# A fused RWKV-5 and tanh-shrink kernel: who issues the first loads, and a planner that counts the two halves' ports

## The chip, the cores and the metric

The kernel runs on one core of one Trainium2 chip. A core has TensorE (PE), VectorE (DVE), ScalarE (ACT), GpSimd (POOL) and SyncE (SP), each with its own queue of instructions in order. Transfers between memory and SBUF are issued here by SP, ACT and POOL and moved by 16 DMA engines. The metric is the device time of one launch in microseconds (us); lower is better.

## The reference

A linear attention with a decaying state, for 4 batches, 8 heads, 768 steps and heads of 48, and then a layer of hidden width 2048 on its 3072 rows of 384:

```python
for t in range(S):
    cur = einsum('bhd,bhe->bhde', u[None] * kt, vt)
    y[:, :, t] = einsum('bhd,bhde->bhe', rt, state + cur)
    state = w[None, :, :, None] * state + einsum('bhd,bhe->bhde', kt, vt)
x = y.transpose(0, 2, 1, 3).reshape(3072, 384)
h = x @ w_in            # 384 x 2048
g = h - tanh(h)
out = g @ w_out         # 2048 x 384
```

r, k, v, w and u are float32. w_in and w_out are float64: the kernel gets them as 64-bit integers and makes float32 of them itself.

## The kernel before

**Units.** The attention is cut into 24 units of 64 steps and two batches; unit n works on steps 64 (n // 2) and on batches 0, 1 or 2, 3. The first batch of a unit lies on SBUF partitions 0 to 63, the second on 64 to 127. `fetch` loads each of r, k and v in two transfers, one for each half (`z` 0 and 1), of 96 KB in runs of 192 bytes. A unit then goes through these steps: PE turns r and k (`turn`, L763), DVE and ACT scale or copy them (`rT` L767, `kT` L771 or L776), PE multiplies them (`levels`, L717), DVE copies the product under a mask into `at` (`x.cp`, L919), ACT writes the diagonal (L788) from `du` (DVE, L780, L909, L784), PE makes the outputs and the new state (`outputs`, `to_state`), ACT takes the outputs into `xt` and `rest` (L855), and DVE updates the state (L882, L928). `kw` (L894) is k with a decay.

A head has 48 numbers and takes 64 partitions, so 16 rows of each half are left; three of the eight heads' worth of output is put there. That is done by copies: POOL's six transfers `xt<-rest` (`fill`, L876) for each pair of units, the "fills". A pair of units makes one block j of 256 rows.

**Hidden tiles.** For each block j, the layer runs in tiles of 256 hidden columns (`hidden`): PE computes h in two groups of six matmuls (L168), ACT makes five functions of it (L177 to L185), DVE combines them to g (L192 to L198), and PE multiplies g by w_out (L206, or L257 in a form with seven products that POOL's sums L242 to L246 and DVE's `mixed` L266 prepare). The first six blocks go through the weights in three passes of 4, 4 and 8 column groups, so that the first hidden tiles need few weights: 12 tiles on the first four weight pieces, 12 on the next four, and 24 on the rest.

**Weights.** There are 16 pieces (w_in and w_out in turn, two of each: n = 0, 1 of w_in, 2, 3 of w_out, and so on), each 768 KB as loaded into one of four staging tiles `st`. A w_out piece is one transfer by SP. A w_in piece comes in four parts: 48 rows at partition 0, 16 rows at 48, 48 rows at 64 and 16 rows at 112. SP loads the two parts of 48 rows, POOL the two of 16 (L123). Five DVE (L137, L138, L141 to L143) and two ACT instructions (L139, L140) convert a piece; the staging tile is then free for the piece four later.

**The planner.** Everything in the main part is a task with an engine, a cost in us, the tasks it must follow and a due time (`add`). `Plan.order` first sets due times backwards from the dependences and then changes them at random many times; each time `forward` lays all tasks out on the engines by these costs, and the change is kept if the laid-out end is no later. In the first part of the search only the time up to `BUSY` is laid out. The instructions are then issued in the order that results, so a cost in the planner moves no instruction's duration, only the order on each queue. For transfers `forward` has one channel that serves them one after the other (`data` us each), a time from issue to landing of at least `LANDS`, `LANDED` after the channel, and 8 transfers under way on each queue (`LANES`). Where PE would wait at the start, dummy matmuls (`fills`, L655) are put in.

Of the kernel before, what the change touches and what calls it, by code (L numbers as in the profile page):

```python
# [33 lines left out]
AHEAD = 2  # L34
# [266 lines left out]
class Plan:  # L301
# [6 lines left out]

    HOP, NEAR_HOP, LANDS, LANDED, LANES, EARLY, SPARE, WARM, SLOW = 0.16, 0.06, 2.4, 1.6, 8, 45.0, 20.0, 6.0, (60.0, 3.0)
    AHEAD, BUSY = 0.05, 240.0  # L310
    CHUNK, CHUNK_0, ASKED, COMES, FIRST = 256, 192, 55, 3.4, 9.5
# [4 lines left out]

    def add(self, engine, cost, run, after=(), due=1e9, data=0, gated=False, steps=0):
        t = SimpleNamespace(engine=engine, cost=cost, run=run, after=[x for x in after if x], due=due, data=data,
                            gated=gated, steps=steps, then=[], n=len(self.tasks))
        for x in t.after:  # L320
            x.then.append(t)
        self.tasks.append(t)
        return t
# [12 lines left out]
    def forward(self, due, until=1e9):  # L336
# [3 lines left out]
        waiting = self.queues(ready, count)  # L340
        free, lanes, channel = dict(self.BEGIN), {}, 0.0
        step, bound, comes, fills = 0, self.CHUNK_0, 0.0, iter(self.fills)
# [3 lines left out]
        while len(done) < len(ready):  # L346
# [40 lines left out]
            if t.data:  # L387
                channel = max(channel, start + 1.2) + t.data
                end = max(end + self.LANDS, channel + self.LANDED) + self.slow(start)
                lanes[e] = lanes[e][1:] + [end]  # L390
# [58 lines left out]

    def order(self, first=2500, tries=500):  # L450
# [12 lines left out]
        def moved():  # L463
            by, at, wide = chance.choice((0.3, 1, 2, 5)), chance.uniform(0, until), chance.choice((15, 40, 100, 700))
            return [x + chance.gauss(0, by) * (start is not None and abs(start - at) < wide / 2) for x, start in zip(due, plan[1])]


        until = self.BUSY
        plan = self.forward(due, until)
        for _ in range(first):  # L470
            new = moved()
            other = self.forward(new, until)
            if other[0] <= plan[0]:
                plan, due = other, new
# [41 lines left out]
def near(ctx, tc, r, k, v, w, u, out, shared, moe_w_in, moe_w_out):  # L516
# [136 lines left out]
    def fills(to):  # L653
# [20 lines left out]
    doubled = add("ACT", .6, lambda: A.copy(twice, inverse[:, :, None, 1:].to_broadcast([128, NP, 2, SHORT])), [now])  # L674
    now = tabled = add("PE", .7, table, [doubled], steps=8)
    downs = add("ACT", .5, lambda: A.copy(w_down, tab.rearrange("s (h d) -> s h d", h=H)[:, :, :D]), [now])
# [6 lines left out]
        out=ub.rearrange("p h d -> p (h d)"),  # L683
        in_=bass.AP(tensor=u.tensor, offset=u.offset, ap=[[0, 128], [1, H * D]])), data=.7)

# [15 lines left out]
    for n in range(weights.count):  # L701

        queues, data = (("SP",), (3.0,)) if n % 4 > 1 else (("SP", "POOL") * 2, (1.2, .95) * 2)
        of = [add(e, .55, lambda n=n, i=i, e=e: weights.load(n, i, e_of[e]), [converted[n - 4] if n >= 4 else None],
                  data=x, gated=True) for i, (e, x) in enumerate(zip(queues, data))]
# [15 lines left out]
    def unit(n):  # L721
# [21 lines left out]
        direct = j == 0  # L743

        def fetch(name, src, after):
            def run(z):
                if name == "k" and not hasattr(t, "kt"):
                    t.kt = first_k[slot] if direct else load.tile([128, H, D], F32, name="kt", tag="kt")
                to = {"r": rt, "v": vt}.get(name)
                Q.dma_start(out=(t.kt if to is None else to)[HALF[z], :, :D],  # L750
                            in_=src[half * 2 + z, :, steps_at, :].rearrange("h t d -> t h d"))

            of = [add("SP", .65, lambda z=z: run(z), after, data=.71) for z in range(2)]
            return add("none", 0, lambda: None, of)
# [135 lines left out]
        if two:  # L890
            free = [b1.xt, b1.rest, b1.add, b1.cp, b1.diag]
        turns, turned = .46, 16
        x.turn = add("PE", turns, lambda: turn(rt, r_ps), [x.r] + free, steps=turned)
# [9 lines left out]
        if product:  # L903
            now = add("ACT", 1.05, own_k, [x.kT, w_us])
            x.own = add("PE", .7, own_levels, [now, x.rT, b2.out], steps=64)
            x.diag = add("DVE", .64, lambda: V.copy_predicated(t.at, same.bitcast(I32)[:, None, None, :].to_broadcast([128, 2, NP, SHORT]), own_lev), [x.own, b2.out])
# [7 lines left out]
        if two:  # L914
            now = add("PE", .66, from_state, both + [x.rT, b1.xt, b1.rest, b1.add, b2.decay, x.kT], steps=64)
            begun = [add("ACT", .15, between, [now])]
        x.lev = add("PE", .7 if two else (1.33 if swap else 1.73) if ch else .7, levels,
                    begun + [x.kT, x.rT, b2.out] + ([b2.decay, b1.xt, b1.rest, b1.add] if ch else []), steps=128 if ch and not two else 64)
        x.cp = add("DVE", .64, lambda: V.copy_predicated(t.at, before, lev), [x.lev, b2.out] + ([] if product else [x.diag]))  # L919
        x.out = now = add("PE", .95 if direct else 1.21, outputs,  # L920
                          [x.cp, x.diag, x.v, b1.xt, b1.rest, b1.add] + ([x.extra] if direct else [x.kw]), steps=96 if direct else 128)
        if direct:
            now = x.out = add("PE", .55, to_state, [now, x.kw], steps=64)
# [3 lines left out]
        x.add = add("DVE" if ch else "ACT", .47 if ch else 1.2, keep, [x.out, x.rest, x.xt]) if more else None  # L927
        x.decay = x.add if not ch else add("DVE", .47, lambda: V.tensor_tensor(state[:, :, :, :D], state[:, :, :, :D], w_all, ALU.mult), [x.add]) if more else None  # L928
        if direct:
            filled.setdefault((j, "all"), []).append(x.xt)  # L930
        elif slot == L - 1:
            filled[j, "all"] = [add("POOL", .52, lambda i=i, kk=kk: fill(i, kk), [x.rest, x.xt], data=.1)
                                for kk in range(NK) for i in range(2)]
# [17 lines left out]
    def finished_seven(t, x, half, due, pace):  # L951
# [9 lines left out]
        for i in (1, 0):  # L961
            now = steps[4 if i else 6]
            if t.fs[0]:
                now = add("DVE", .47, lambda i=i: dense.gather(t, i), [now], due + 3 * pace)
            stored[j, i] = [add("POOL", .6, lambda z=z, i=i: dense.store(t.os[i], L * j + i, z, G), [now], due + 4 * pace, data=.4)
                            for z in range(2)]

    def hidden(j, fs, f, due, pace, seven=False):
# [40 lines left out]
        for i in range(L):  # L1009
# [7 lines left out]
            if whole and j < d.NB - 1:  # L1017

                stored[j, i] = [add("POOL", .6, lambda z=z, i=i, ends=ends: dense.store(ends.o, L * j + i, z, G),
                                    [x.empty[-1]], due + 4 * pace, data=.4) for z in range(2)]  # L1020

# [339 lines left out]
```

## Time and profile before

| | before |
|---|---|
| runs | 603.26, 606.02 and 605.67 us, median 605.67 |
| profiled execution | 607.26 us, of which the span from first to last instruction is 605.5 |
| busy PE, DVE, ACT, POOL | 582.4, 466.4, 403.3, 201.0 us |
| mean granted TensorE clock | 0.989 |
| DMA | 33.78 MB in 86326 packets, 78536 of them under 512 B |

"Busy" is time in which an engine executes something. An engine that waits is not busy, but PE's matmuls are pipelined with modelled ends, so a busy PE may be waiting between them. DMA share is the mean share of time in which the 16 DMA engines had a packet under way. "A <- B" in a list of waits means that A stood idle until B let it go. Six matmuls of h at full clock take 1.29 us when they follow each other closely, and 1.49 to 1.56 when a group stands alone.

### The profile page before, as it was taken

To read this page: it belongs to the slowest core of one execution; us is meant where nothing else is said; L and a number is where in the kernel's file an instruction comes from. 1 tells how busy PE (TensorE), PEld (TensorE's weight loads), DVE (VectorE), ACT (ScalarE), POOL (GpSimd) and SP (SyncE) were. 2 spreads that over 40 slices of the span, in tenths; PEclk is the share of its full clock that TensorE was granted. 3 is DMA by queue.
4 is the path that set the end of the run, shared out by engine and by line. 5 is a ranking of instruction groups with operands and counts; after the bars stand their busy time and mean duration, and the time that the engine had idled before them with its cause. 6 is when DMAs were issued, how large, how long until landed. Compare 5 with 4: busy or idle time off the path is not lost.

```text
span 605.5 us, 14670 instructions
## 1 busy us (share of the span) xinstructions
PE 582.4 (96%) x5781; PEld 485.7 (80%) x5781; DVE 466.4 (77%) x782; ACT 403.3 (67%) x902; POOL 201.0 (33%) x366
## 2 busy tenths in 40 slices
PE   8877999999999999999999999999999999999996
PEld 4555767667777669999999999888889889889995
DVE  6699699999999999867677776767765775555666
ACT  3677699899866676655556686465866676565652
POOL 5002212021000123544455473425334435334540
PEclk9889899999999999999999999999999999999999
DMA  6966585967300210110111020122201100100101
GB/s 125 228 126 126 113 194 99 143 167 124 105 14 0 48 28 14 26 27 1 28 27 26 2 60 1 41 41 48 53 16 34 41 2 8 29 2 8 26 3 30
DMA packets 86326, 33.78 MB, mean 56 GB/s; under 512 B 78536, under 2 KB 80680, under 8 KB 86248
## 3 DMA queue, kind: packets, MB, share of 16 engines
q1 hardware_dynamic: 81084, 25.57, 21.1%
q0 software_dynamic: 4992, 6.99, 5.5%
q8 instruction: 47, 0.77, 0.5%
q14 instruction: 31, 0.25, 0.2%
q10 hardware_dynamic: 172, 0.20, 0.1%
HBM read 26.94 MB, written 4.72 MB: 52 GB/s over the span
## 4 chain that ended last, share of the span: by engine, by line
PE 76%; DVE 6%; DMA 5%; ACT 4%; issue 4%; SPq 3%; POOL 1%; DVEq 0%; ACTq 0%; POOLq 0%
PE h L168 37%; PE p L257 26%; PE o L206 6%; PE yk_ps L717 4%; SPq L750 3%; DMA st<-in_moe_w_in_dram 2%; DMA xt<-rest 1%; PE yk_ps L763 1%; POOL xt L876 1%; DMA st<-in_moe_w_out_dram 1%; DVE rT L767 1%; DVE at L919 1%; ACT s L177 1%; DVE tg L194 1%; DVE g L198 1%
## 5 line engine op out<-in xcount | busy, mean ns | idle before, releaser
L168 PE MATMUL h<-xt,w_in_sb 128*128 128x256 f32 x1152 | 285.7, 385 | 2.7 <-DMA xt<-rest 2.7
L168 PEld LDWEIGHTS h<-xt,w_in_sb 128*128 128x128 f32 x1152 | 214.6, 192 | 35.9 <-issue 2.1
L242 POOL TENSOR_TENSOR sg<-g 128x256 f32<-128x256 f32 x69 | 52.1, 755 | 176.7 <-DVE g L198 152.2
L257 PE MATMUL p<-mixed,sg 128*128 128x192 f32 x426 | 104.1, 326 | 0.0
L192 DVE TENSOR_TENSOR g<-h,th 128x512 f32<-128x512 f32 x96 | 65.8, 686 | 48.9 <-ACT s L177 23.0
L194 DVE SCALAR_TENSOR_TENSOR tg<-s,tg 128x512 f32<-128x512 f32 x96 | 71.1, 741 | 36.6 <-ACT tg L181 20.0
L181 ACT ACTIVATE tg<-h 128x512 f32<-128x512 f32 x96 | 57.2, 596 | 58.5 <-PE h L168 56.9
L179 ACT ACTIVATE th<-h 128x512 f32<-128x512 f32 x96 | 57.4, 598 | 39.1 <-PE h L168 39.0
L177 ACT ACTIVATE s<-h 128x512 f32<-128x512 f32 x96 | 57.4, 598 | 37.3 <-PE h L168 37.2
L876 POOL DMA_DIRECT2D xt<-rest x66 | 32.5, 499 | 146.3 <-ACT rest L855 145.8
L257 PEld LDWEIGHTS p<-mixed,sg 128*128 128x128 f32 x426 | 75.0, 190 | 0.3 <-issue 0.3
L198 DVE COPY_PREDICATED g<-small,tg 128x512 f32<-128x512 int32 x96 | 71.1, 741 | 4.7 <-DVE tg L196 0.5
L257 PE MATMUL p<-w_out_sb,g 128*128 128x192 f32 x284 | 71.9, 335 | 1.1 <-DVE at L919 1.1
L196 DVE SCALAR_TENSOR_TENSOR tg<-q,tg 128x512 f32<-128x512 f32 x96 | 67.5, 703 | 6.4 <-ACT q L183 2.4
L206 PE MATMUL o<-w_out_sb,g 128*128 128x384 f32 x192 | 71.3, 495 | 0.1
L183 ACT ACTIVATE q<-s,m1b 128x512 f32<-128x512 f32 x96 | 69.8, 727 | 0.6
L185 ACT ACTIVATE small<-s,smallb 128x512 f32<-128x512 f32 x96 | 69.6, 725 | 0.3
L257 PEld LDWEIGHTS p<-w_out_sb,g 128*128 128x128 f32 x284 | 51.8, 190 | 9.0 <-DVE at L919 1.5
L788 ACT ACTIVATE at<-same,du 128x64 f32<-128x64 f32 x184 | 47.9, 343 | 2.8 <-DVE du L784 2.6
L206 PEld LDWEIGHTS o<-w_out_sb,g 128*128 128x128 f32 x192 | 35.2, 190 | 15.8 <-DVE g L198 0.2
L246 POOL TENSOR_TENSOR sg<-sg,g 128x128 f32<-128x128 f32 x69 | 41.0, 594 | 5.1
L244 POOL TENSOR_TENSOR sg<-sg,g 128x128 f32<-128x128 f32 x69 | 36.6, 530 | 5.2
(133 smaller groups left out, 672.3 us busy)
## 6 DMA issues: line engine op xcount, KB each, us to landing
st<-in_moe_w_out_dram SPq DMA_DIRECT2D x8, 768.0 KB, 4.5
rt<-in_r_dram SPq DMA_DIRECT2D x48, 96.0 KB, 2.9
vt<-in_v_dram SPq DMA_DIRECT2D x48, 96.0 KB, 3.4
st<-in_moe_w_in_dram SPq DMA_DIRECT2D x16, 288.0 KB, 5.5
kt<-in_k_dram SPq DMA_DIRECT2D x44, 96.0 KB, 3.1
out_dram<-o POOLq DMA_DIRECT2D x44, 96.0 KB, 2.2
st<-in_moe_w_in_dram POOLq DMA_DIRECT2D x16, 96.0 KB, 6.0
xt<-rest POOLq DMA_DIRECT2D x66, 16.0 KB, 2.1
```

What stands on the lines that cost most here:

```text
L168: self.nc.tensor.matmul(t.h2[:, z], self.w_in_sb[:, t.f // 2, kk, z * 128 : (z + 1) * 128], self.xts[t.j][:, kk].rearrange("p b t -> p (b ...
L177: A.activation(out, t.h, AF.Square)
L179: A.activation(out, t.h, AF.Tanh)
L181: A.activation(out, t.h, AF.Tanh, scale=G1)
L183: A.activation(out, t.s, AF.Square, bias=self.m1b)
L185: A.activation(out, t.s, AF.Relu, bias=self.smallb, scale=-1.0)
L192: V.tensor_tensor(t.g, t.h, t.th, ALU.subtract)
L194: V.scalar_tensor_tensor(t.tg, t.s, C4, t.tg, ALU.mult, ALU.mult)
L196: V.scalar_tensor_tensor(t.tg, t.q, K1, t.tg, ALU.add, ALU.mult)
L198: V.copy_predicated(t.g, t.small.bitcast(I32), t.tg)
L206: self.nc.tensor.matmul(self.outs[i], t.g2[:, z, i * C : (i + 1) * C], self.w_out_sb[:, t.f + z, :], start=t.first and z == 0, stop=t.last ...
L257: self.nc.tensor.matmul(ps[bank][:, half * n : (half + 1) * n], a, b, start=t.first and half == 0, stop=t.last, skip_group_check=True)
```

## The change

It moves two kinds of transfers to other queues and gives the planner another picture of transfers, with new figures.

- The 48 rows of w_in at partition 64 are loaded by POOL and the 16 rows at 112 by SP. POOL so loads one part of each size per piece, and SP too.
- The second batch (`z` 1) of r, k and v of units 0 and 1 is loaded by ACT, six transfers. All others stay on SP.
- In the planner each queue has a time `ring` at which its last transfer was served, and each half of the partitions has a port: a transfer with a `side` takes `HALF` x `data` on its half's port.
- Costs: r, k and v 0.28 us of the channel for each half instead of 0.71, w_out pieces 2.5 instead of 3.0, w_in parts 0.82 and 0.4 instead of 1.2 and 0.95; several PE costs are lower (turns 0.38 instead of 0.46, outputs 0.97 instead of 1.21); ACT's `own_k` is 1.2 instead of 1.05.
- The search starts four times, each with 2000 changes laid out up to 110 us, and goes on from the best with 300 changes of the whole; before it was one start of 2500 up to 240 us, and 500.

```diff
-    HOP, NEAR_HOP, LANDS, LANDED, LANES, EARLY, SPARE, WARM, SLOW = 0.16, 0.06, 2.4, 1.6, 8, 45.0, 20.0, 6.0, (60.0, 3.0)
-    AHEAD, BUSY = 0.05, 240.0
+    HOP, NEAR_HOP, LANDS, LANDED, LANES, EARLY, SPARE, WARM, SLOW = 0.16, 0.06, 2.1, 1.35, 8, 45.0, 20.0, 6.0, (60.0, 1.5)
+    AHEAD, BUSY, STARTS = 0.05, 110.0, 4
+    HALF = 1.75
...
             if t.data:
-                channel = max(channel, start + 1.2) + t.data
-                end = max(end + self.LANDS, channel + self.LANDED) + self.slow(start)
+                begin = max(start + 1.4, ring.get(e, 0.0))
+                channel = max(channel, begin) + t.data
+                ring[e] = channel
+                if t.side is not None:
+                    ports[t.side] = max(ports[t.side], begin) + self.HALF * t.data
+                    ring[e] = max(channel, ports[t.side])
+                end = max(end + self.LANDS, ring[e] + self.LANDED) + self.slow(start)
...
-        until = self.BUSY
-        plan = self.forward(due, until)
-        for _ in range(first):
-            new = moved()
-            other = self.forward(new, until)
-            if other[0] <= plan[0]:
-                plan, due = other, new
+        until, begun, best = self.BUSY, due, None
+        for _ in range(self.STARTS):
+            due = begun
+            plan = self.forward(due, until)
+            for _ in range(first):
+                new = moved()
+                other = self.forward(new, until)
+                if other[0] <= plan[0]:
+                    plan, due = other, new
+            if best is None or plan[0] < best[0]:
+                best = plan[0], due
+        due = best[1]
...
-        queues, data = (("SP",), (3.0,)) if n % 4 > 1 else (("SP", "POOL") * 2, (1.2, .95) * 2)
+        queues, data, sides = (("SP",), (2.5,), (None,)) if n % 4 > 1 else (("SP", "POOL", "POOL", "SP"), (.82, .4, .82, .4), (0, 0, 1, 1))
...
+        def queue(z):
+            return "SP" if not z else "ACT" if n < 2 else "POOL" if n < 2 else "SP"
...
-                Q.dma_start(out=(t.kt if to is None else to)[HALF[z], :, :D],
+                e_of[queue(z)].dma_start(out=(t.kt if to is None else to)[HALF[z], :, :D],
...
-            of = [add("SP", .65, lambda z=z: run(z), after, data=.71) for z in range(2)]
+            of = [add(queue(z), .65, lambda z=z: run(z), after, data=.28, side=z) for z in range(2)]
```

More of the change, by code (lines that the diff above doesn't have):

```diff
@@ L315, in __init__, with add @@
         self.tasks, self.fills = [], []
-    def add(self, engine, cost, run, after=(), due=1e9, data=0, gated=False, steps=0):
+    def add(self, engine, cost, run, after=(), due=1e9, data=0, gated=False, steps=0, side=None):
         t = SimpleNamespace(engine=engine, cost=cost, run=run, after=[x for x in after if x], due=due, data=data,
-                            gated=gated, steps=steps, then=[], n=len(self.tasks))
+                            gated=gated, steps=steps, side=side, then=[], n=len(self.tasks))
         for x in t.after:
@@ L340, in forward @@
         waiting = self.queues(ready, count)
-        free, lanes, channel = dict(self.BEGIN), {}, 0.0
+        free, lanes, channel, ring, ports = dict(self.BEGIN), {}, 0.0, {}, [0.0, 0.0]
         step, bound, comes, fills = 0, self.CHUNK_0, 0.0, iter(self.fills)
@@ L448, in backward, with order @@
         return latest
-    def order(self, first=2500, tries=500):
+    def order(self, first=2000, tries=300):
         due = [t.due for t in self.tasks]
@@ L674, in near @@
     doubled = add("ACT", .6, lambda: A.copy(twice, inverse[:, :, None, 1:].to_broadcast([128, NP, 2, SHORT])), [now])
-    now = tabled = add("PE", .7, table, [doubled], steps=8)
+    now = tabled = add("PE", .5, table, [doubled], steps=8)
     downs = add("ACT", .5, lambda: A.copy(w_down, tab.rearrange("s (h d) -> s h d", h=H)[:, :, :D]), [now])
@@ L683, in near @@
         out=ub.rearrange("p h d -> p (h d)"),
[L684 removed]
+        in_=bass.AP(tensor=u.tensor, offset=u.offset, ap=[[0, 128], [1, H * D]])), data=.5)
     add("ACT", 1.3, lambda: A.activation(fixed("warm", [128, 1]), shared["one"], AF.Tanh), due=0)
@@ L701, in near @@
     for n in range(weights.count):
-        queues, data = (("SP",), (3.0,)) if n % 4 > 1 else (("SP", "POOL") * 2, (1.2, .95) * 2)
+        queues, data, sides = (("SP",), (2.5,), (None,)) if n % 4 > 1 else (("SP", "POOL", "POOL", "SP"), (.82, .4, .82, .4), (0, 0, 1, 1))
         of = [add(e, .55, lambda n=n, i=i, e=e: weights.load(n, i, e_of[e]), [converted[n - 4] if n >= 4 else None],
-                  data=x, gated=True) for i, (e, x) in enumerate(zip(queues, data))]
+                  data=x, gated=True, side=side) for i, (e, x, side) in enumerate(zip(queues, data, sides))]
         if weights.sources[n % 4 > 1].dtype != I64:
@@ L891, in unit @@
             free = [b1.xt, b1.rest, b1.add, b1.cp, b1.diag]
-        turns, turned = .46, 16
+        turns, turned = .38, 16
         x.turn = add("PE", turns, lambda: turn(rt, r_ps), [x.r] + free, steps=turned)
@@ L903, in unit @@
         if product:
-            now = add("ACT", 1.05, own_k, [x.kT, w_us])
-            x.own = add("PE", .7, own_levels, [now, x.rT, b2.out], steps=64)
+            now = add("ACT", 1.2, own_k, [x.kT, w_us])
+            x.own = add("PE", .5, own_levels, [now, x.rT, b2.out], steps=64)
             x.diag = add("DVE", .64, lambda: V.copy_predicated(t.at, same.bitcast(I32)[:, None, None, :].to_broadcast([128, 2, NP, SHORT]), own_lev), [x.own, b2.out])
@@ L914, in unit @@
         if two:
-            now = add("PE", .66, from_state, both + [x.rT, b1.xt, b1.rest, b1.add, b2.decay, x.kT], steps=64)
+            now = add("PE", .58, from_state, both + [x.rT, b1.xt, b1.rest, b1.add, b2.decay, x.kT], steps=64)
             begun = [add("ACT", .15, between, [now])]
-        x.lev = add("PE", .7 if two else (1.33 if swap else 1.73) if ch else .7, levels,
+        x.lev = add("PE", .6 if two else (1.06 if swap else 1.46) if ch else .56, levels,
                     begun + [x.kT, x.rT, b2.out] + ([b2.decay, b1.xt, b1.rest, b1.add] if ch else []), steps=128 if ch and not two else 64)
         x.cp = add("DVE", .64, lambda: V.copy_predicated(t.at, before, lev), [x.lev, b2.out] + ([] if product else [x.diag]))
-        x.out = now = add("PE", .95 if direct else 1.21, outputs,
+        x.out = now = add("PE", .86 if direct else .97, outputs,
                           [x.cp, x.diag, x.v, b1.xt, b1.rest, b1.add] + ([x.extra] if direct else [x.kw]), steps=96 if direct else 128)
         if direct:
-            now = x.out = add("PE", .55, to_state, [now, x.kw], steps=64)
+            now = x.out = add("PE", .5, to_state, [now, x.kw], steps=64)
         x.xt = add("ACT", .96 if swap else .4, to_xt, [now, last_h.get(j - FIRST - 2) if slot == 0 else None])
@@ L926, in unit @@
             x.rest = add("ACT", .62 if swap else .26, to_rest, [x.xt] + (filled.get((j - 2, "all"), []) if slot == 0 else []))
-        x.add = add("DVE" if ch else "ACT", .47 if ch else 1.2, keep, [x.out, x.rest, x.xt]) if more else None
+        x.add = add("DVE" if ch else "ACT", .47 if ch else .95, keep, [x.out, x.rest, x.xt]) if more else None
         x.decay = x.add if not ch else add("DVE", .47, lambda: V.tensor_tensor(state[:, :, :, :D], state[:, :, :, :D], w_all, ALU.mult), [x.add]) if more else None
@@ L931, in unit @@
         elif slot == L - 1:
-            filled[j, "all"] = [add("POOL", .52, lambda i=i, kk=kk: fill(i, kk), [x.rest, x.xt], data=.1)
+            filled[j, "all"] = [add("POOL", .52, lambda i=i, kk=kk: fill(i, kk), [x.rest, x.xt], data=.1, side=i)
                                 for kk in range(NK) for i in range(2)]
@@ L964, in finished_seven @@
                 now = add("DVE", .47, lambda i=i: dense.gather(t, i), [now], due + 3 * pace)
-            stored[j, i] = [add("POOL", .6, lambda z=z, i=i: dense.store(t.os[i], L * j + i, z, G), [now], due + 4 * pace, data=.4)
+            stored[j, i] = [add("POOL", .6, lambda z=z, i=i: dense.store(t.os[i], L * j + i, z, G), [now], due + 4 * pace, data=.3)
                             for z in range(2)]
@@ L1019, in hidden @@
                 stored[j, i] = [add("POOL", .6, lambda z=z, i=i, ends=ends: dense.store(ends.o, L * j + i, z, G),
-                                    [x.empty[-1]], due + 4 * pace, data=.4) for z in range(2)]
+                                    [x.empty[-1]], due + 4 * pace, data=.3) for z in range(2)]
     for n in range(L * (FIRST + 2)):
```

## The prediction

> **What bounds the kernel now.** I read the windows first, in three cuts. The columns are the stretch, then busy us and instructions of PE, PE's weight load, DVE, ACT and POOL, then granted clock, DMA share and GB/s.
>
> ```profile
> 0.00:230.00 230.00, 211.74 (x2820) 150.51 (x2821) 207.13 (x352) 170.06 (x411) 38.28 (x92) 0.97 0.54 108
> 230.00:590.00 360.00, 359.89 (x2911) 326.38 (x2910) 249.69 (x412) 228.74 (x483) 162.73 (x275) 1.00 0.11 24
> ```
>
> From 230 to 590 us PE is busy for 359.89 of 360: there the change can gain nothing. All of it is decided before 230 us, and there DVE is busy for 207.1 us, so it is idle for 22.9. PE's own 211.7 hides its losses: 17.9 of them are dummy matmuls (L655), and matmuls that start late or run at a low clock count as busy too. So the start is bound by DVE, which converts the 16 weight pieces (five instructions each) beside the units' and the hidden tiles' work. Where is it idle?
>
> ```profile
> 0.00:10.00 10.00, 8.00 (x37) 4.00 (x39) 5.97 (x15) 3.51 (x8) 7.33 (x33) 1.00 0.48 96
> 10.00:20.00 10.00, 7.70 (x202) 4.97 (x202) 5.27 (x11) 4.32 (x17) 1.53 (x4) 1.00 1.10 170
> 20.00:30.00 10.00, 8.57 (x175) 6.44 (x176) 8.22 (x14) 5.70 (x16) 0.57 (x1) 0.83 1.02 265
> 60.00:70.00 10.00, 9.70 (x162) 7.38 (x158) 5.34 (x10) 5.07 (x16) 0.76 (x2) 0.69 0.36 72
> ...
> 2.00:4.00 2.00, 2.00 (x4) 0.87 (x4) 0.99 (x3) 1.48 (x2) 2.00 (x11) 1.00 0.17 33
> 8.00:10.00 2.00, 1.52 (x16) 0.82 (x14) 1.77 (x3) 1.24 (x4) 1.04 (x2) 1.00 0.77 156
> 18.00:20.00 2.00, 1.50 (x14) 0.60 (x13) 0.29 (x1) 0.31 (x2) 0.00 (x0) 1.00 1.19 168
> ```
>
> Idle DVE by tens: 4.0, 4.7, 1.8, and 4.7 at 60 to 70; 15.2 of the 22.9 lie in these four. The DMA engines have room up to 10 us (share 0.17 to 0.77) and none from 10 to 30. The chain of waits and the timeline say what DVE waited for.
>
> ```profile
> 10.28 0.62 SPq L123
> 10.94 8.65 DMA st<-in_moe_w_in_dram
> 19.71 0.56 DVE L137 TENSOR_SCALAR power<-st 128x768 uint32<-128x768 uint32 x1 [2.91 <-DMA st<-in_moe_w_in_dram]
> 35.59 0.95 DVE L143 TENSOR_TENSOR w_in_sb<-w_in_sb,power 128x768 f32<-128x768 f32 x1
> 52.37 0.72 DVE L919 COPY_PREDICATED at<-before,x_ps 128x512 f32<-128x512 int32 x1
> 52.54 6.17 DMA xt<-rest
> 61.33 2.92 PE L168 MATMUL h<-xt,w_in_sb 128*128 128x256 f32 x6
> ```
>
> The first piece of w_in is issued at 10.28 and 10.94, behind 11 of the 12 r, k, v halves of units 0 and 1 on SP's queue, lands at 19.6, and DVE starts on it at 19.71. Piece 1 is converted by 36.5, unit 4's mask copy (L919) runs at 52.4. Then the third hidden tile waits 6.17 us for the fills xt<-rest, which POOL issued beside its next w_in loads; it runs at 61.3 to 64.3, its six matmuls taking 2.92 us where 1.56 is usual (clock 0.69 in that ten).
>
> **The change, part by part.** The program of the changed kernel shows the order on each queue; the durations are the rows of before.
>
> *SP and ACT.* Ahead of the first w_in load SP issued 12 transfers after that of w (2.1 to 10.2 us, 0.66 apart); now 7 are left, so it is issued at about 2.1 + 7 x 0.66 + some waiting = 7.5. ACT takes six. No row shows an r, k or v issue on ACT; the nearest are its two final stores:
>
> ```profile
> L1328 ACTq DMA_DIRECT2D out_dram<-last x2: 580/622/663, 600.7 to 601.5; - x2
> 1.20 1.28 ACTq L661 DMA_DIRECT2D rows<-in_u_dram  x1
> ```
>
> I take 0.62, as on SP (0.60 to 0.64); 1.28, the launch's first, is the upper end, and nothing would make it a gain. Three issues stand before the table load, which moves from 2.5 to 4.5 us; ACT's next work needs the column transpose (5.3), so this costs 0.7. Two more stand before w_up, and each waits for the landing of the transfer eight before it, as the eight semaphores are shared: I find 6.3 and 7.0. Behind them w_up comes at 7.6 instead of 6.7, and twice at 8.9 instead of 8.5; DVE is in its reciprocal until 8.3 anyway. At 1.28 each, w_up would come at 11 and all that follows some 3 us later.
>
> *POOL.* Per w_in piece it issues one 48-row and one 16-row load where it issued two of 16 rows: the same 16 instructions in another size. The 16-row loads take 0.52, the one-row-per-partition fills 0.48 (16 rows), the stores 0.54 (64 rows); from the last two, an estimate for 144 runs is 0.63, at most 0.1 more for each, under POOL's 145.8 us of waiting for ACT's rest. Nothing is gained there.
>
> *The first piece's landing.* A rule of the Trainium skill speaks against a gain here: "DMA: Bandwidth & Descriptors", section "Issuing engines are not separate DMA queues", says that all issuers share the same 16 DMA engines, so another issuer saves only issue time. The rows from 10 us on (share 1.06 to 1.19) agree that the engines are full then; but the first rows (0.17 to 0.77) leave room, and at full share these w_in bytes move at about 170 GB/s, while 20 to 30, with the w_out loads, shows 265. Two 48-row loads for different halves behind each other on one queue may be what is slow. By the rule the piece comes 10.3 - 7.5 = 2.8 us sooner, at 16.8; by the rows, where the halves now stand on two queues, 4 to 5 sooner. I take 15 to 15.5; by the rule alone the sum below is some 1.5 us less.
>
> *DVE from there*, by its new order and the pitches of the trace (0.47 for 384 columns, 0.61 and 0.65 for 512, 0.47 and 0.87 for 768): after rT and kT of unit 0 (8.3 to 9.6) it waits for r and k of unit 1 until 10.7, twelve instructions (5.1 us) end at 15.8, and the first conversion starts there, not at 19.7. In it stand kw, rk, rT and du of unit 2 and the first steps of piece 1: piece 0 is done at 24.1 (24.9 before), piece 1 after six more instructions (4.2 us) at 28.3 (36.5 before); w_out's first piece at 35, unit 3's mask copy at 35.6, and after twelve more (6.5 us) unit 4's at 42.3, against 52.4. These need w_out's first piece by 24.7: to then 18 halves (1.73 MB), u, two w_in pieces and two w_out pieces, 5.0 MB, must be moved, which before took until 30; from 3.5 us on at 230 GB/s it is 25.
>
> *The fills.* Pieces 4 and 5 of w_in are now loaded before the first fill on POOL, not between fills. So unit 3's rest (ACT at about 38) is filled and landed by 38.6 + 3 + 2.7 = 44.3, and the third hidden tile runs at about 45 to 46.5, with PE not cooled by an idle ten. Of DVE's idle time the 4.7 at 60 to 70, 3.9 at 10 to 20 and 1.8 at 20 to 30 go: 10.4 us.
>
> *The rest of the start.* Unit 12 moves from ahead of the 11th hidden tile to behind the 19th. Ahead of the 28th tile's h, which ends at 230.1 before, DVE has 329 planned instructions instead of 337: six of mixing, one kw and one g fewer, 7 x 0.47 + 0.6 = 3.9 us less. But at the 11th tile it has 98.6 us of work behind it, not 108.0, and by the 26th nearly as much as before (184.0 and 185.2): in between 85.4 us of DVE stand beside 83.3 of PE. That overload (2.1) and waits like the 2 us from 200 to 230 give back about 4.
>
> *All else* (other planner figures, four starts of the search) moves instructions only in the start; from the 36th tile on the DVE and PE work ahead of a tile is the same. The last 15 us keep their waits.
>
> **Sum.** 10.4 + 3.9 - 4 = 10.3 us off the span of 605.5: 595.2. The profiled execution took 607.26, 1.8 over its span, and the median of the runs is 605.67, 1.6 under it; so 605.67 - 10.3 = 595.4, said as 595. If nothing is given back it is 591; if only half of the idle time goes, 600.
>
> **Rivals.**
> *It is given back (22%).* DVE is 97% busy from 130 to 230 whatever comes before, so an earlier start only moves its idle time to the middle. For it: the overload worked out above; PE was busy for 9.9 of 10 us in most tens from 130. Against it: the instructions themselves are fewer by 3.9. Then about 4 us remain: 601.5.
> *Slower (13%): r, k and v held behind staged weights on SP.* A w_in or w_out load waits until the piece four before it is converted, and whatever stands behind it on SP waits too; the longest such wait of before is 9.2 us (25.5 in six). Now pieces 4 and 5 stand on SP between unit 3's v and units 4's and 5's r and k, and ACT's issues and loads share the eight semaphores. If piece 1's conversion ends later than about 38 us (28 by my working), unit 5's k lands after DVE wants it, and each us there holds all units behind. Two waits of 8 us against the 10 gained: 605.7 + 16 - 10 = 612.
> *It does nothing at the landing (5%).* The engines are full anyway, piece 0 comes at 19, and the new order is as good as the old: 605.5. Against it: two of the five first tens have DMA share well under 1.
>
> **How the numbers follow.** The forecast has 60%, with a range of its own from 588 to 601. For the whole, 587 to 606: it takes in the case of time given back and the unchanged one, leaves out the slower case and the best of the forecast. This kernel's measurement can tell about 0.5%, 3 us, from no change: under 602.6 lie nearly all of the forecast and two thirds of the given-back case (0.74), over 608.7 the slower case and a little (0.14), between them 0.12.
>
> **What would show it.** Right: L137's first instruction at 15 to 16.5; the second hidden tile's h done before 31; no wait of PE for xt<-rest over 1 us; clock near 1.00 from 60 to 70; DVE busy for more than 195 of the first 215 us. Wrong: w_up after 9 us; the first L137 after 18; L750 or L123 on SP with a wait of over 5 us before 60; PE idle between 110 and 230 by more than 4 us. The prediction as a whole fails if PE is not full by about 220 us.

## The result, and the profile after

| | before | after |
|---|---|---|
| median of 12 runs each, us | 605.41 (603.26 to 608.95) | 603.09 (598.99 to 605.45) |
| ratio, 95% interval | 1 | 0.995 (0.9929 to 0.997) |
| profiled execution and its span, us | 607.26, 605.5 | 600.33, 598.6 |

The change gains 0.5%, about 3 us, where 10.3 were forecast. The two traces differ by more, 6.9 us, and that has a reason of its own, which the last group of experiments shows. First the windows of the kernel after, with the columns as before.

```profile
0.00:10.00 10.00, 7.31 (x28) 3.91 (x29) 4.69 (x13) 2.15 (x4) 6.60 (x33) 1.00 0.70 120
10.00:20.00 10.00, 7.48 (x173) 5.59 (x172) 6.38 (x13) 4.36 (x16) 2.37 (x5) 0.83 1.19 170
20.00:30.00 10.00, 6.47 (x132) 4.79 (x132) 6.10 (x11) 5.12 (x15) 0.00 (x0) 0.66 1.16 248
60.00:70.00 10.00, 10.00 (x212) 7.35 (x203) 9.92 (x19) 9.66 (x29) 2.62 (x6) 1.00 0.48 93
0.00:230.00 230.00, 214.88 (x2865) 157.38 (x2866) 209.07 (x355) 175.69 (x421) 42.17 (x97) 0.98 0.55 108
230.00:590.00 360.00, 359.65 (x2909) 326.03 (x2908) 252.69 (x420) 227.96 (x481) 157.35 (x269) 1.00 0.11 24
```

The last row is as it was: nothing is won behind 230 us. The fourth is what was hoped for: DVE is busy for 9.92 of 10 us from 60 to 70, where it was 5.34, and the clock is 1.00 instead of 0.69. The first three are not. From 0 to 10 us there was room and it was used, 120 GB/s instead of 96; but the share of the DMA engines from 10 to 20 went from 1.10 to 1.19, and the rate stayed at 170 GB/s; and DVE is now idle for 3.9 us from 20 to 30, where it was 1.8. The timeline of the kernel after shows why (start, duration, instruction, and in brackets the idle time before it with what ended it):

```profile
8.40 0.34 SPq L123 DMA_DIRECT2D st<-in_moe_w_in_dram  x1
...
9.38 0.62 ACT L683 COPY w_up<-power 128x512 f32<-128x512 f32 x1 [3.20 <-DMA vt<-in_v_dram]
...
14.39 0.56 DVE L796 TENSOR_TENSOR rk<-rt,first_k 128x384 f32<-128x384 f32 x1 [3.06 <-DMA rt<-in_r_dram]
...
19.82 0.54 DVE L137 TENSOR_SCALAR power<-st 128x768 uint32<-128x768 uint32 x1
...
20.39 0.56 PE L729 MATMUL x_ps<-rT,kT 48*64 48x64 f32 x19
...
22.83 0.56 DVE L910 TENSOR_TENSOR kw<-kt,w_down 128x384 f32<-128x384 f32 x1 [2.00 <-DMA kt<-in_k_dram]
...
24.47 0.69 PE L729 MATMUL x_ps<-rT,kT 48*64 48x64 f32 x13 [3.53 <-issue]
```

SP's first w_in load is issued at 8.40 instead of 10.28. But the first conversion (L137) starts at 19.82, where it was 19.71. Before, it waited for its piece; now its row has no idle time before it. The last part of the piece landed at 18.9, and DVE was busy until 19.82 with the ten instructions from 14.39 on, which had waited for r of unit 1. ACT stood for 3.20 us in front of w_up, since its k, r and v transfers wait in its queue for earlier ones to land; the second half of unit 1's r, which DVE needs first, was issued by ACT at 8.71 and landed at 14.27; and PE stopped for 3.53 us in the middle of 32 matmuls with nothing to wait for ("issue").

### The profile page after: what moved, and what is told of

It reads as the page before. It is cut to its first block, busy times and chain, and to the rows that moved or that the text cites. A ratio compares the mean times of both kernels' runs of the same rounds, so it can differ in the third digit from the quotient of the medians.

```text
span 598.6 us, 14643 instructions
## 1 busy us (share of the span) xinstructions
PE 578.1 (97%) x5783; PEld 485.3 (81%) x5783; DVE 465.5 (78%) x782; ACT 403.6 (67%) x902; POOL 199.5 (33%) x366
## 4 chain that ended last, share of the span: by engine, by line
PE 86%; DMA 5%; DVE 3%; SPq 2%; issue 1%; ACT 1%; ACTq 0%; POOL 0%; DVEq 0%; POOLq 0%
PE h L168 41%; PE p L257 26%; PE o L206 9%; PE yk_ps L729 6%; SPq L766 2%; DMA vt<-in_v_dram 2%; DMA kt<-in_k_dram 1%; PE x_ps L779 1%; PE x_ps L729 1%; PE yk_ps L779 1%; DMA rt<-in_r_dram 1%; DMA xt<-rest 1%; PE p L206 0%; DVE rT L783 0%; DVE at L935 0%
## 5 line engine op out<-in xcount | busy, mean ns | idle before, releaser
L242 POOL TENSOR_TENSOR sg<-g 128x256 f32<-128x256 f32 x69 | 52.4, 759 | 165.5 <-DVE g L198 149.6
L892 POOL DMA_DIRECT2D xt<-rest x66 | 32.3, 494 | 126.5 <-ACT rest L871 125.6
L246 POOL TENSOR_TENSOR sg<-sg,g 128x128 f32<-128x128 f32 x69 | 39.3, 569 | 5.0
L244 POOL TENSOR_TENSOR sg<-sg,g 128x128 f32<-128x128 f32 x69 | 36.8, 534 | 5.0
```

## The experiments

Each kernel ran beside the kernel before on its chip; a ratio is to that, with the 95% interval. "First h" is the start of the first hidden tile; the expectations mean the start of its second group of six matmuls, 27.3 in before and 37.0 in after.

### Queues or order

The change has two parts that can be had apart: who issues two groups of transfers, and the order that the new planner makes. In e3 the new order keeps all old queues, in e4 the old order has the new queues, in e1 and e2 only one of the two groups of transfers goes back.

```diff
 e1 and e3, from after
-                e_of[queue(z)].dma_start(out=(t.kt if to is None else to)[HALF[z], :, :D],
+                Q.dma_start(out=(t.kt if to is None else to)[HALF[z], :, :D],
 e2 and e3, from after
-        of = [add(e, .55, lambda n=n, i=i, e=e: weights.load(n, i, e_of[e]), ...
+        of = [add(e, .55, lambda n=n, i=i, e=e: weights.load(n, i, e_of[('SP', 'POOL', 'SP', 'POOL')[i]]), ...
 e4, from before: the same two lines the other way round, (A if z and n < 2 else Q) and ('SP', 'POOL', 'POOL', 'SP')
```

> The changed kernel's order on every engine, but each transfer issued by the queue it had before (SP for all r, k, v; SP for both 48-row parts of w_in, POOL for both 16-row parts). Theory A (the gain comes from the new order after 60 us; the DMA engines are full until 40 us whoever issues): time as the changed kernel's, 601 to 604, first hidden tile at 35 to 40 us. Theory B (the new queues bring the gain, the order alone would lose): 606 to 612, first hidden tile after 41. Theory C (the new queues fill the DMA engines and starve PE's instruction fetch, so they cost): faster than the changed kernel, 596 to 600, waits of PE for issue before 40 us under 2 us in sum instead of 6.6.

> The order of before, with the new queues: second batch of r, k, v of units 0 and 1 on ACT, 48 rows at partition 64 on POOL, 16 rows at 112 on SP. Theory A: as before, 604 to 607, first hidden tile within 2 us of 27.3. Theory B: faster, 598 to 602, first conversion before 17.5. Theory C: slower, 607 to 611, with waits of PE for issue before 40 us of over 3 us where before had 0.7.

> The changed kernel with only the six transfers of ACT put back on SP, at the same place in the order. Theory A: 601 to 604. Theory B, if ACT's issues are what helps: 605 to 609, unit 1's r and k landing 2 us later. Theory C, if ACT's issues are what starves the fetch: 597 to 600.

> The changed kernel with only w_in's parts put back (both of 48 rows on SP, both of 16 on POOL). Theory A: 601 to 604. Theory B, if the two halves of 48 rows beside each other are what helps: 604 to 608, piece 0 landing 2 us or more after the changed kernel's. Theory C, if POOL's queue takes a larger share of the DMA engines with 288 KB parts and holds up r and k of unit 2 on SP's: 597 to 600, with the first transfer of unit 2's r landing in under 9 us instead of 11.6.

| kernel | median us | ratio |
|---|---|---|
| e3, new order, old queues | 599.77 | 0.9916 (0.9888 to 0.9943) |
| e4, old order, new queues | 606.10 | 1.0018 (0.9985 to 1.0052) |
| e1, r, k, v back on SP | 600.72 | 0.9915 (0.9882 to 0.9949) |
| e2, parts of w_in as before | 602.37 | 0.9944 (0.9917 to 0.9971) |

All of the gain is the order's. The new queues bring nothing to the old order, and ACT's six transfers cost the new one about a third of a per cent: without them it is at 0.9915, with them at 0.995. The intervals of this one pair overlap; of two later pairs with the same difference, e13 and e10 (0.9905 and 0.997) have intervals that do not meet, and e15 and e14 runs that do not overlap. Crossing the parts of w_in does nothing (0.9944 without it). Theory C fails by its own sign: PE's stop called "issue" took 4.3 us in e3, where it had to be under 2, and 2.2 in e4, where it had to be over 3, though e3's time lies in C's range.

In e1, SP issues the second half of unit 1's r at 9.14 and it lands at 11.78, and w_up runs at 6.74; in after these are 8.71, 14.27 and 9.38. It is so in nine traces of the new order: on SP this half is issued at 8.9 to 9.1 and lands at 11.5 to 11.8 (e1, e3, e13, e15), on ACT it is issued at 8.6 to 9.2 and lands at 14.3 to 16.9 (after, e2, e10, e12, e14). So the transfer that is wanted first lands later on another queue, beside weights, though it is issued at about the same time. In e1 the weights pay in turn: DVE begins unit 1 earlier, at 11.90, and then waits 4.81 us for its first piece.

```profile
6.74 0.62 ACT L683 COPY w_up<-power 128x512 f32<-128x512 f32 x1 [0.57 <-DVE power L680]
...
11.90 0.56 DVE L796 TENSOR_TENSOR rk<-rt,first_k 128x384 f32<-128x384 f32 x1 [2.25 <-DMA rt<-in_r_dram]
...
22.16 0.56 DVE L137 TENSOR_SCALAR power<-st 128x768 uint32<-128x768 uint32 x1 [4.81 <-DMA st<-in_moe_w_in_dram]
```

### Does the load go faster on two queues?

e9 computes nothing. It issues the start's loads in groups, each when the one before has landed, and goes through the whole list twice in its one run.

```diff
+            for parts in ([(0, Q), (2, Q)], [(0, Q), (2, G)], [(0, Q), (2, A)], [(0, Q), (1, G), (2, Q), (3, G)], [(0, Q), (1, G), (2, G), (3, Q)]):
+                for i, q in parts:
+                    weight(n, i, q)
+                done(0, True)
...
+            for q in (Q, A):
+                for i in range(8):
+                    for z in range(2):
+                        half(i, z, q if z else Q)
+                done(8)
```

> Only loads, nothing computed (the output is zeros): groups of the start's transfers, each group issued when the one before has landed and DVE has read it, the whole list twice with other pieces. Per list: the two 48-row parts of a w_in piece (590 KB) on SP and SP, on SP and POOL, on SP and ACT; a whole w_in piece (786 KB) as before (SP both 48-row parts) and as after (crossed); a w_out piece (786 KB) on SP; 16 halves of r, k, v (1.57 MB) all on SP, then one half of each pair on ACT; 8 halves of partitions 0 to 63 alone (786 KB) on SP, then every second one on ACT; both 48-row parts beside 8 halves, the parts on SP and then on POOL. Theory A (the 16 DMA engines set the rate whoever issues, and what is asked for together shares it): from first issue to last landing each pair of a group with the same bytes differs by less than 10%, or by no more than the issue time that is saved where the engines are not yet full; w_in alone moves at 170 to 200 GB/s on one queue and on two. Theory B (the prediction's: two 48-row loads for different halves behind each other on one queue are what is slow): SP and POOL, or SP and ACT, land the 590 KB at least 1 us sooner than SP and SP. In either case the halves' 16 issues at 0.62 us on one queue take 9.9 us, against 5 on two, so if the engines carry 230 GB/s the split list lands in 7 to 8.5 us instead of 11 to 12; if they carry 170 in runs of 192 bytes, in 10.5.

Windows cut from first issue to last landing of the groups in the second round (DVE, POOL, clock, DMA share, GB/s): the two 48-row parts on SP and SP, SP and POOL, SP and ACT; a whole w_in piece as before and as after; 16 halves of r, k, v on SP, then on SP and ACT; 8 halves of one side on SP, then on SP and ACT; 8 halves and two 48-row parts, the parts ahead on SP, then beside them on POOL.

```profile
126.60:132.20 5.60, 0.05 (x2) 0.00 (x0) 1.00 0.53 105
133.10:138.50 5.40, 0.02 (x1) 0.58 (x1) 1.00 0.54 109
139.30:144.10 4.80, 0.04 (x2) 0.00 (x0) 1.00 0.49 123
145.00:151.70 6.70, 0.00 (x0) 1.02 (x2) 1.00 0.60 117
152.60:159.00 6.40, 0.04 (x2) 1.09 (x2) 1.00 0.62 123
...
164.80:178.10 13.30, 1.54 (x16) 0.00 (x0) 1.00 0.65 119
178.70:190.40 11.70, 1.51 (x15) 0.00 (x0) 1.00 1.06 135
191.00:198.70 7.70, 1.48 (x15) 0.00 (x0) 1.00 0.55 102
199.30:207.10 7.80, 1.55 (x16) 0.00 (x0) 1.00 0.84 101
208.10:217.90 9.80, 0.62 (x5) 0.00 (x0) 1.00 1.02 140
218.40:228.70 10.30, 1.05 (x13) 1.15 (x2) 1.00 0.87 134
```

From first issue to last landing the two parts took 5.43, 5.29 and 4.68 us, the whole piece 6.61 and 6.27 (6.21 and 6.67 in the first round of the list). With ACT they land 0.75 sooner, about the 0.4 that SP needs between two issues and a little more; with POOL, which the change uses, 0.14. The 16 halves took 13.2 us on one queue and 11.6 on two, the 8 halves of one side 7.7 on both. With two queues the halves land 0.59 us apart (0.68 where all go to one side), and SP alone issues one every 0.68. So one queue nearly keeps up with the landings, and a second took 13.2 down to 11.6, no further. Theory A holds. The last two groups show the price: with the parts on POOL the whole takes 10.2 us instead of 9.75, and the second to sixth half, which land 2.7 to 3.4 us after their issue where halves are alone, land after 3.9 to 4.8 with the parts ahead on SP and after 5.2 to 6.1 with them beside on POOL. See also the share: 0.65 and 1.06 stand for 119 and 135 GB/s, 0.55 and 0.84 for 102 and 101. So a share under 1 need not be room, and a larger one need not be speed: it counts the time in which a packet is under way, and in the last pair of figures more of it moved no more bytes.

### How much of the order's gain is luck?

The search is random. e5 is e3, and e6 is the kernel before, with `Random(6)` and `Random(7)` instead of 5. e8 tells the new planner of the old queues, so that it plans for what e3 only did.

```diff
-        chance = Random(5)
+        chance = Random(6)
 e8, from after
-        queues, data, sides = ... (("SP", "POOL", "POOL", "SP"), (.82, .4, .82, .4), (0, 0, 1, 1))
+        queues, data, sides = ... (("SP", "POOL", "SP", "POOL"), (.82, .4, .82, .4), (0, 0, 1, 1))
-            return "SP" if not z else "ACT" if n < 2 else "POOL" if n < 2 else "SP"
+            return "SP"
```

> The changed planner with another seed of its random search (6 instead of 5), all transfers on their old queues as in the order-only kernel. Theory A1 (the new figures and the ports make a better order, whatever the seed): within 3 us of the order-only kernel's 599.8, that is 597 to 603, clearly under the old planner with the same seed. Theory L (the search is a lottery, and seed 5 drew well): anywhere from 598 to 612, overlapping the old planner's seeds.

> As with seed 6, with seed 7. Theory A1: 597 to 603. Theory L: 598 to 612.

> The planner and kernel of before with seed 6. Theory A1: 604 to 612, as seed 5 of before. Theory L: anywhere from 598 to 612.

> The planner and kernel of before with seed 7. Theory A1: 604 to 612. Theory L: 598 to 612.

> The new planner told of the old queues (r, k, v all on SP, w_in's 48-row parts on SP), so that the order is made for them. Theory A1: as the order-only kernel, 597 to 603. If the order made for the new queues is needed for the gain: 604 or more.

New planner, old queues: 0.9916, 0.997 (0.9941 to 0.9998), 0.9908 (0.9878 to 0.9938), and planned so 0.9888 (0.985 to 0.9925). Old planner: 1, 0.997 (0.9942 to 0.9999), 1.0003 (0.9972 to 1.0033). The new one is better on the mean of these few, and one seed in three gives it no lead: with seed 6 it took 604.11 us, outside theory A1's range. About 0.6% hangs on the seed, more than the whole change was worth. What in the new planner does it, its figures, its two ports or its longer search, was not taken apart.

### Less to load at the start

If the engines are what holds the start, 576 KB less should free it. In e7 (from after) and e7b (from e3) units 0 and 1 load four of the eight heads; DVE sets the others to zero, in lines that are left out here.

```diff
-            e_of[queue(z)].dma_start(out=(...)[HALF[z], :, :D],
-                        in_=src[half * 2 + z, :, steps_at, :].rearrange("h t d -> t h d"))
+            e_of[queue(z)].dma_start(out=(...)[HALF[z], : (4 if n < 2 else H), :D],
+                        in_=src[half * 2 + z, : (4 if n < 2 else H), steps_at, :].rearrange("h t d -> t h d"))
```

> The changed kernel, but units 0 and 1 load only four of the eight heads of r, k and v (the rest is set to zero by six small DVE memsets of about 0.2 us, beside DVE's early idle time): 576 KB of 192-byte runs less in the first 20 us; heads 4 to 7 of the first 64 steps are left out. Theory D (the DMA engines are what holds the start): the first hidden tile comes 3 us or more sooner, at 34 or before, instead of 37.0 to 40.5, and the wait of PE for issue in the first levels of unit 1 shrinks from 3.5 to under 1.5 (PE's instructions are fetched by the same engines); time 597 to 600. Theory I (issue order and waits on shared semaphores hold the start, not the bytes): the first tile within 1.5 us of 37, time within 1 us of the changed kernel's 603.

> The same half loads of units 0 and 1 in the order-only kernel (old queues). Theory D: first hidden tile at 31 to 32 instead of 34.7; time 595 to 598 against its 599.8. Theory I: 34 to 35, time 599 to 600.5.

0.9938 (0.9912 to 0.9964) and 0.9891 (0.9833 to 0.9949): within the intervals of after and e3. First h came at 33.7 in e7 (34.7 in after) and at 35.7 in e7b (32.3 in e3); counted as in the expectations, 36.2 for 37.0 and 38.0 for 34.7. A miss: fewer bytes alone did not bring the start forward, as theory D wanted, so the landings are not its only bound. D's other sign came: PE's stop ahead of unit 1's levels fell to 1.0 us in e7. But PE stopped again later, in sum by the "issue" rows 3.1 us in e7 and 4.2 in e7b; what those stops are is read in the section on the hardware.

### Where the rest of the gain goes

The changed kernel's first trace is 6.9 us shorter than before's, the medians only 2.3. So I ran it again beside two more (e12). The other two were to move one 768 KB load of w_out out of the way of POOL's fills.

```diff
 e10 (from after) and e13 (from e1); e14 and e15 the same with n == 7
-        of = [add(e, .55, lambda n=n, i=i, e=e: weights.load(n, i, e_of[e]), ...
+        of = [add(e, .55, lambda n=n, i=i, e=e: weights.load(n, i, G if n == 6 else e_of[e]), ...
```

> The changed kernel itself again, so that the two beside it are compared on one chip. Every theory: ratio to before 0.993 to 0.997, 602 to 604 us. Theory F (the third hidden tile's wait for its fills has moved to a later tile's, where it is short or long by chance, because POOL issues the last of six fills at 69.8 us, just behind SP's 786 KB load of a w_out piece at 69.4): the new trace may show the wait h<-xt<-rest near 74 us with anything from 0.6 to 4 us, and the longer it is the longer is the execution. Theory G (nothing happens there in most executions, the difference between 600.3 of the traced one and 603.1 of the median is spread over many small waits): the wait is again under 1 us in a trace of 602 us or more.

> The changed kernel with one load moved: the w_out piece that SP issues at 69.4 us is issued by POOL, in whose queue it stands behind the six fills xt<-rest of 67.0 to 69.8. Theory F: no wait of PE for xt<-rest over 0.3 us near 74, the clock is 1.00 from 70 to 90, the last fill lands within 3 us of its issue and not 4.8 (or 7.3, as in the run with the old parts' queues), and the median falls by 2 to 4 us against the changed kernel run beside it, to 599 to 601. Theory G: the median is within 1 us of the changed kernel's. Against both, if DVE wants that piece before 77 us, the later load costs up to 1 us.

> The same moved load, and ACT's six transfers of r, k and v back on SP's queue, which by itself gave 0.9915. Theory F: the wait of 1.8 us for xt<-rest and the clock of 0.83 from 70 to 80 that the run with only r, k, v on SP's queue showed are gone, ratio 0.986 to 0.990, 597 to 599 us. Theory G: 0.9915 again.

e12: 602.44 us, 0.9942 (0.992 to 0.9964), and this time its trace is of 604.76 us. Its timeline, and its waits of PE from 60 to 90 (total, times, longest):

```profile
69.56 1.91 POOL L892 DMA_DIRECT2D xt<-rest  x4 [0.31 <-issue]
...
70.17 0.58 SPq L123 DMA_DIRECT2D st<-in_moe_w_out_dram  x1
...
74.68 0.70 PE L168 MATMUL h<-xt,w_in_sb 128*128 128x256 f32 x2
...
77.72 1.36 PE L168 MATMUL h<-xt,w_in_sb 128*128 128x256 f32 x4 [2.34 <-DMA xt<-rest]
```

```profile
PE h L168 <- DMA xt<-rest: 2.3, 1, 2.3
```

SP issues the load at 70.17, between POOL's last fills: those issued at 70.51 and 70.99 landed after 5.4 and 6.6 us, the four ahead of it after 1.9 to 3.4. PE begins the fifth tile's h and stands in it for 2.34 us; in the windows from 70 to 90 the clock is then 0.91 and DVE busy for 15.71 of 20 us, where the first trace of the same kernel has 1.00 and 18.86. In that one only the last fill was behind the load (landing after 4.8 us, a wait of 0.6); in e2's trace, of 605.39 us, the wait was 3.6.

e10 and e13 missed their aim. SP issues the w_out loads of this stretch in the order 7, 6, and I had moved piece 6, which comes later; the last fills still landed after 5.3 to 6.6 us. 0.997 (0.995 to 0.9989) and 0.9905 (0.9869 to 0.994): the first no better than after, the second as e1. e14 and e15 move piece 7.

> The changed kernel with the other w_out load moved, the one that SP does issue at 69.4 to 70.7 us between POOL's last fills (the two runs before had moved the next one, of 74 us, and the last fills still landed after 5.3 to 6.6 us): POOL issues it now, behind the six fills. Theory F: the last fills land within 3.2 us of their issue, no wait of PE for xt<-rest over 0.3 us between 60 and 90, clock 1.00 from 70 to 90, the fifth and sixth hidden tiles' h done at 85 or sooner after a fourth at 68 to 69 (90.0 where the wait was 2.3), and 0.4 to 0.7% off the changed kernel's 0.9942: 0.987 to 0.991, 598 to 600.5 us. Theory G: 0.994 again, within 0.2%.

> The same load moved, and ACT's six transfers of r, k and v on SP's queue. Theory F: no wait for xt<-rest over 0.3 us between 60 and 90, 0.985 to 0.989, 596.5 to 599 us. Theory G: 0.9915, as with r, k, v on SP's queue alone.

The timeline of e14, and its window from 70 to 90 (PE, weight load, DVE, ACT, POOL, clock, share, GB/s) after that of e12:

```profile
69.79 1.92 POOL L892 DMA_DIRECT2D xt<-rest  x4 [0.32 <-issue]
...
71.69 0.78 POOL L123 DMA_DIRECT2D st<-in_moe_w_out_dram  x1
...
74.90 1.56 PE L168 MATMUL h<-xt,w_in_sb 128*128 128x256 f32 x6
```

```profile
70.00:90.00 20.00, 17.43 (x331) 12.20 (x334) 15.71 (x30) 14.41 (x45) 3.20 (x8) 0.91 0.68 158
```

```profile
70.00:90.00 20.00, 19.78 (x474) 14.61 (x472) 19.60 (x37) 18.60 (x56) 5.36 (x11) 1.00 0.78 175
```

The fills land after 2.3 to 3.0 us, the six matmuls of the fifth tile follow each other, and 3.9 us of DVE's idle time are gone. e14: 600.65 us, 0.9892 (0.9869 to 0.9914), against 0.9942 (0.992 to 0.9964) for after: the intervals do not meet. Its six times lie within 2.4 us, the twelve of after within 6.5. e15, without ACT's six transfers too: **598.37 us, 0.9856 (0.9829 to 0.9884)**, the best version, ahead of both kernels; its four times lie between 598.30 and 598.44, all below the six of e14. Theory F held in the wait, in the clock and in the time. Ends of h of the first, fourth, sixth, 28th and last hidden tile (us, from the traces):

| | 1st | 4th | 6th | 28th | 96th |
|---|---|---|---|---|---|
| before | 28.9 | 77.1 | 94.7 | 230.1 | 593.4 |
| after, first trace | 40.5 | 67.8 | 85.3 | 222.2 | 586.2 |
| after again (e12) | 40.5 | 69.0 | 90.0 | 226.8 | 590.8 |
| e14 | 40.8 | 69.2 | 86.0 | 222.8 | 586.8 |
| e15 | 38.5 | 66.9 | 83.6 | 220.5 | 584.5 |

Behind the sixth tile the distances hardly change any more: after and e12 differ by 4.7 there and by 4.6 at the end.

## Why the prediction was wrong, point by point

**The bound** was read rightly: before 230 us, with DVE's idle time as the measure. How that time moved, in us of DVE idle, worked out from the windows of before and the first trace of after:

| | 0-10 | 10-20 | 20-30 | 30-60 | 60-70 | 70-230 | sum |
|---|---|---|---|---|---|---|---|
| before | 4.0 | 4.7 | 1.8 | 1.6 | 4.7 | 6.1 | 22.9 |
| forecast to go | 0 | 3.9 | 1.8 | 0 | 4.7 | -4 | 6.4 |
| after | 5.3 | 3.6 | 3.9 | 4.3 | 0.1 | 3.7 | 20.9 |

**SP, ACT, POOL.** SP's first w_in load at 7.5: it was 8.40, since it waited for a transfer of ACT, r of 3.26, which took 5.12 us to land. ACT's transfers at 0.62: they took 0.61 to 0.71, that was nearly right. But their waits were counted up to 7.0 us; the last ended at 8.7, and w_up at 7.6 became 9.38. POOL's 48-row load took 0.59 to 0.85 us beside 0.52 for one of 16 rows, so "at most 0.1 more" was a little low, with no consequence.

**The landings are the step that failed:** that of unit 1's r, said at 10.7 and measured at 14.27, and that of the first piece, said at 15 to 15.5 and measured at 18.9. The first of the two set the conversion's start in after. I set the rows against the rule of the Trainium skill ("DMA: Bandwidth & Descriptors", "Issuing engines are not separate DMA queues") and took the rows' side: that a share of 0.17 to 0.77 is room and that two halves on one queue are slow. The runs say that the rule was right: 170 GB/s from 10 to 20 us before and after, e9's 6.61 against 6.27 us for a piece, e4's 1.0018. The room up to 10 us was there, but 24 GB/s more for 10 us is 0.24 MB, a third of a piece. The 230 GB/s from 3.5 us on that the sum needed were not reached: after moved 120, 170 and 248 GB/s in its first three tens. Even the value "by the rule alone", 16.8, was too good, because I had moved one transfer forward and left all others where they were. What shares the engines shares the delay: the w_in parts that SP and POOL issued between 8.4 and 11.6 us landed 5.0 to 10.1 us later, those of 14.0 and 16.4 9.6 to 9.8 us later, and unit 1's r and unit 2's k with them.

**DVE from there** was a chain on those landings: first conversion 15.8 (it was 19.82, and 22.81 in e12, the same kernel), piece 0 done at 24.1 (31.5), piece 1 at 28.3 (37.9), unit 4's mask copy at 42.3 (53.4, and 52.4 in before). Of the 5.7 us of idle time that should go from 10 to 30 us, 1.1 went and 2.1 came; and 4.0 came beside them, at 0 to 10 and 30 to 60. In sum DVE lost 5.0 us up to 60.

**The fills.** "Loaded before the first fill, so the wait at 61 goes": it went, with DVE busy and the clock at 1.00 from 60 to 70. The time of the third tile, 45 to 46.5, was wrong: its h ended at 59.6, and until 56.7 PE had units' work and dummy matmuls instead. But the prediction asked of every step what is late next, and not of this one: the fifth tile's fills meet SP's load of w_out, 0.6 us of waiting in one trace and 2.3 in the other. e14 prices it: 0.9942 against 0.9892, half a per cent, 3 us.

**The rest of the start.** Up to the end of the 28th tile's h, DVE is busy for 207.2 us in before and 201.3 in after: 5.9 us of work now stand behind that tile, where 3.9 were forecast. The idle time up to there went from 22.9 to 20.9 in the first trace, and to 25.6 in e12, with the same work. The 4 us of idle time that an overload between the 11th and the 26th tile was to give back did not come: PE has no wait from 110 to 230 us, where before has 3.6. The lead does shrink there, from 11.0 us at the 11th tile's end to 7.5 at the 26th's, but by work: PE is busy throughout.

**The sum.** Forecast -5.7 (landing) - 4.7 (fills) - 3.9 (order) + 4 (given back). Shown: idle time -2.0 in the first trace and +2.7 in the second, work -5.9 and -6.0, and 0.7 more behind the 28th tile in both. So what is gained is the order's work, and of the 10.4 us of idle time little or nothing. In its parts: about nothing for the landing, and some 0.3% paid for ACT's transfers (e1 against after, e15 against e14); the fills' 4.7, of which some 3 are on the median paid back two tiles later (e14 against e12); and the order's part without its return. The rival "given back" came nearer in size, 601.5 where 603.1 was measured, and had the place wrong: DVE's idle time from 70 to 230 us fell from 6.1 to 3.7. The slower rival, SP's staged weights, had its wait: SP stood 3.37 us at 16.36, and kt of unit 2 came late by 2.0 for DVE; not 16.

**The signs.** Two of those for being wrong came, w_up after 9 us and the first L137 after 18; the two others, a long wait of SP and idle time of PE behind 110, did not. Of those for being right the clock from 60 to 70 came, and the fills' wait under 1 us in the first trace only. The second tile's h was done at 43.9, not before 31, and DVE was busy for 194.5 us of the first 215, not more than 195.

## What to carry to other kernels

A queue in order was also a priority here: unit 1's r landed 2.6 us after its issue on SP's queue and 5.6 beside the weights on ACT's. Whatever is sent earlier on another queue shares the engines with what is wanted first, so ask of every transfer moved forward which landing it delays, and by its bytes at the measured rate. When a wait is removed, look for the next transfer of the same kind and for what large load is issued beside it; in e12 a 16 KB fill issued 0.3 us behind a 768 KB load landed after 5.4 us instead of 1.9 to 3.4, and a queue order (both on one queue) is a cheap way to put it ahead. And look at more than one execution before a trace is explained: the same kernel's two traces differed by 4.4 us, 3.5 of it in one place.

## What the runs showed of the hardware that I had not expected

PE's stops called "issue" come at a fixed place in its program. Counting matmuls in the records, PE stopped ahead of the 221st in after and in twelve other kernels (e1, e2, e3, both e5, e6 with seed 6, e7, e7b, e10, e13, e14 and e15), whatever instruction that is (one or two later in before, e4, e8 and e6 with seed 7), and then in some of them of the 348th and 475th. That is every 127 matmuls, and with their weight loads 256 instructions: the 449th, 705th and 961st. The Trainium skill ("Runtime: NRT & Kernel Launch", "Instruction fetch mechanics") has instructions fetched in blocks of 256 by a DMA queue of the engine, and calls the crossing mostly hidden. Here is the block under way in after, in the DMA view from 21 to 22 us (packets, MB, share):

```profile
q1 hardware_dynamic: 391, 0.15, 126.0%
q8 instruction: 1, 0.02, 9.3%
```

The place and the one packet of 16 KB fit the page; that it is hidden does not. The stop took 0.7 us in before, 3.5 in after, 4.3 in e3, 6.7 in e15, and these rows show the most of it (e15's waits of PE, then before's):

```profile
PE x_ps L729 <- issue: 6.7, 1, 6.7
```

```profile
PE x_ps L717 <- issue: 0.7, 1, 0.7
```

In all 18 traces of the whole kernels PE goes on 1.3 to 1.8 us after the end of the first such packet: the packet ends at 16.69 and PE goes on at 18.14 in before, 22.92 and 24.47 in after, 22.35 and 24.09 in e15. So the stop is a wait for the block. The packet takes 1.2 to 1.6 us everywhere; what differs is when it begins, 15.17 in before and 21.44 in after. Reaching the place sooner gains little then: e12, the same kernel as after, began its 94th matmul at 18.63 instead of 15.90, stopped for only 0.3 us, and began its 221st at 24.73 where after did at 24.47. That would be why e1 and e7 gain less at the first tile than their landings promise. Why the block begins late, by the full DMA engines or by the point at which it is asked for, was not tested, as no run changed its transfer alone. My sum had no such term.
